# Attention units spread over more steps of token blocks 1 and 2, and the given stores moved behind the last weight load

## The chip, the core and the metric

The kernel runs on one core of a Trainium2 chip. The metric is the device time of one execution in microseconds (us), the median of three runs. The core's engines work side by side, each through its own instructions in order: TensorE (PE, matrix products), VectorE (DVE), ScalarE (ACT), GpSimd (POOL) and SyncE (SP, which here issues transfers). They wait for each other through semaphores.

## What is computed

Attention inside chunks of 64 tokens, for 8 batches, 8 heads, 576 tokens and a head width of 64, and then a gated layer over the 4608 tokens:

```python
scores = scale * np.matmul(q_c, k_c.transpose(0, 1, 2, 4, 3))    # 64 x 64 in each chunk
scores = scores - np.max(scores, axis=-1, keepdims=True)
attn = np.exp(scores)
attn = attn / (np.sum(attn, axis=-1, keepdims=True) + 1e-09)
out = np.matmul(attn, v_c)
...
x = np.ascontiguousarray(attn_out.transpose(0, 2, 1, 3)).reshape(B * S, H * D)   # 4608 x 512
gate = 1.0 / (1.0 + np.exp(-(x @ w_gate)))                       # 512 x 1536
val = x @ w_val                                                  # 512 x 1536
return (gate * val @ w_out).astype(np.float32)                   # 1536 x 512
```

## The kernel before

The 4608 tokens are nine blocks (m = 0 to 8) of 512. The attention of a block is four *units* j (4m to 4m+3), handled two at a time. The 1536 hidden columns are twelve *slices* f of 128. Each weight is held as a high and a low float part, so every product takes three matmuls per 128 rows.

**Words used below.** A *step* is `step(m, f, span)`: slice f of a block's hidden values, 12 matmuls for the gate, 12 for the value (`up`, L277), a sigmoid on ACT (L286 in block 0, L302 in blocks 1 and 2) and a product on DVE (L288 or L304). A step over all 512 tokens has 24 matmuls of 512 columns; an `a` or `b` step covers 256 tokens. *S j* is the scores' products of units j and j+1 (L172, 64 matmuls of 64 columns on PE, written `sc`); *A j* is their products with the values (L243, written `av`).

**Stages.** Block 0 runs while the weights arrive: `START` and `MIDDLE` are strings of operations run by `run(op)`. W is a weight load (L102, issued by SP), C a weight conversion (ACT L123, L124, L130; DVE L125, L126, L128, L131), H a step, D a down projection, L and V loads of q, k and v, K a store of an output weight from POOL (`keep_outer`), G two times three stores of converted up weights from SP (`keep_given`, the *given stores*). The string `MIDDLE` ends with steps of block 1 in halves: H1.0a to H1.3a, H1.0b to H1.3b. Then `singles` runs the rest of block 1 (slices 4 to 11) and all of block 2 (0 to 11), and `pair` runs the down projection of these two blocks (L660) and the later blocks in pairs.

**What sets the order.** In `MIDDLE` PE and SP keep the order of the string, while the other engines are ordered by a scheduler; in `singles` every engine keeps the written order. The attention of units 8 and up is the generator `flow()`, cut into pieces: S, two transposes (L737) that take the scores out of their banks and a maximum (L741); an exchange of halves on ACT (L720); maximum and subtraction (L745, L746) and the exponential on ACT (L748, with a table load before and one back to the sigmoid behind it); then A of the unit pair before; sums (L764), exchange, L768, reciprocal (L771), product (L772), two transposes (L776). `tick(share)` adds a credit twice in each step and runs DVE pieces as the credit pays for them; `insert(upto, 1)` runs an S, or an A of a unit below `upto`. `SHARES` holds the credit of a tick in blocks 1 and 2.

**What can wait.** The banks of `sc` and `av` are one pool of two (`psa`): A j waits until L737 has taken the scores of S j+2 out, and S waits until the results of the A before it are copied out (L263 on ACT and L264 on DVE for blocks below 3, L260 on ACT after that). The half steps of block 1 write the banks `g0` and `g1`, of which there is one each: a gate waits for the sigmoid of the step before it, a value for its L304. The full steps of blocks 1 and 2 write `acc`, of which there are four. POOL makes sums of weights (`keep_sums`: L402, L381, L384, L385 and a store) one after the other in the same stretch.

Of the kernel before, what the change touches and what calls it, by code (L numbers as in the profile page):

```python
# [16 lines left out]
D = 64  # L17
# [15 lines left out]
H0.5 D W5o L6 C5.2 L7 C6.2 H0.6 V4 W8u C7.1 D W7o C8.0 t5 C8.1 C7.2 H0.7 D K0 K6 W9u  # L33
"""
MIDDLE = """
C9.0 W8o C8.2 W9o C9.1 W10u A4 K1 K7 H0.8 W10o D C10.0 C9.2 C10.2 W11u G0 H0.9 C10.1 K2 K8 D H0.10 C11.0 G1 C11.1 D
W11o H0.11 G2 K3 K9 S7 V7 S6 D L9 E6 H1.0a C11.2 D V6 E7 H1.1a T6 T7 K4 K10 H1.2a A6 H1.3a H1.0b L8 V8 K5 K11 H1.1b V9 H1.2b H1.3b
"""

VECTOR_TRANSPOSES = 8  # L40

# [4 lines left out]

FIRST_STEP = 4

SHARES = {1: 1.7, 2: 1.8, "up": 1.0, "turned": 0.36}


@with_exitstack
def chunk_attn_moe(ctx: ExitStack, tc: tile.TileContext, q, k, v, w, out, turned_out):
# [39 lines left out]
    def load_weights(f, kind):  # L93
        if kind == "o":
            raws[f, 2] = stage("spare" if f == NF - 1 else f"o{NF - 1 if f == NF - 2 else NF - 1 - f % 2}", 1024)
        elif f == NF - 1:
            raws[f, 0], raws[f, 1] = stage(f"o{f}", 1024), stage("spare", 1024)
        else:
            raw = stage(f"u{NF - 1 if f == NF - 2 else NF - 1 - f % 2}", 2048)
            raws[f, 0], raws[f, 1] = raw[:, :1024], raw[:, 1024:]  # L100
        for part in (2,) if kind == "o" else (0, 1):
            nc.sync.dma_start(raws[f, part], w[f, :, part * 1024:(part + 1) * 1024])  # L102
# [35 lines left out]
    def load(j):  # L138
        m, h, u = units[j]
        state[j] = {}  # L140
        for name, src in (("qt", q), ("kt", k)):
            t = state[j][name] = ap2.tile([P, 2, 256], F32, name=name)
            nc.sync.dma_start(t, src[2 * m + h, u].rearrange("p (a n) -> p a n", a=2))

    def load_values(j):
        m, h, u = units[j]
        vt = ap2.tile([P, 2, 2, 2, D], F32, name="vt")
        nc.sync.dma_start(vt, v[2 * m + h, u].rearrange("p (i a t d) -> p i a t d", i=2, a=2, t=2))
        state[j]["vt"] = vt
# [29 lines left out]
    def scores(j, on_scalar=False):  # L179
        n, i = divmod(j, 2)  # L180
        if n not in pairs:
            pr = early[:, n] if n < 2 else ap2.tile([P, 2, 8, D], F32, name="pr", bufs=1)
            pairs[n] = dict(sc=products(2 * n, n == 1), pr=pr, sums={})
        s = pairs[n]
        scv, pr = s["sc"][i].rearrange("p (g k) -> p g k", k=D), s["pr"][:, i]
        mx = sm.tile([P, 8], F32, name="mx")
        nc.vector.reduce_max(out=mx, in_=scv, axis=AX.X)
        if not on_scalar:
            nc.vector.tensor_tensor(out=pr, in0=scv, in1=mx.unsqueeze(2).broadcast_to([P, 8, D]), op=ALU.subtract)
            return  # L190
        nc.vector.tensor_scalar_mul(out=mx, in0=mx, scalar1=-0.125)
        sums = s["sums"][i] = sm.tile([P, 8], F32, name="sums")
        for g in range(8):
            nc.scalar.activation(
                pr[:, g], scv[:, g], AF.Exp, scale=0.125, bias=mx[:, g:g + 1], accum_out=sums[:, g:g + 1])

    def softmax(j):
        n, i = divmod(j, 2)
        pr = pairs[n]["pr"][:, i]
        sums = pairs[n]["sums"].get(i)  # L200
        if sums is None:
            nc.scalar.activation(pr, pr, AF.Exp, scale=0.125)
            sums = sm.tile([P, 8], F32, name="sums")
            nc.vector.reduce_sum(out=sums, in_=pr, axis=AX.X)
        nc.vector.tensor_scalar_add(out=sums, in0=sums, scalar1=1e-9)
        inv = sm.tile([P, 8], F32, name="inv")
        nc.vector.reciprocal(out=inv, in_=sums)
        nc.vector.tensor_tensor(out=pr, in0=pr, in1=inv.unsqueeze(2).broadcast_to([P, 8, D]), op=ALU.mult)
# [4 lines left out]
    def transposes(j, on_scalar=False):  # L213
        n, u = divmod(j, 2)
        s = pairs[n]
        if u == 0:
            s["pt"] = turned()
        tp = bank("tp", n == 0)
        for i in range(2):
            for t in range(2):  # L220
                g = 4 * u + 2 * t
                nc.tensor.transpose(
                    tp[:, (2 * i + t) * P:(2 * i + t + 1) * P],
                    s["pr"][:, i, g:g + 2].rearrange("p c k -> p (c k)"), ident)
        pt = s["pt"][:, :, u].rearrange("p i t a q -> p i (t a q)")
        tp = tp.rearrange("p (i n) -> p i n", i=2)
        if on_scalar:
            nc.scalar.copy(pt, tp)
        else:
            nc.vector.tensor_copy(pt, tp)  # L230
# [552 lines left out]
    def advance():  # L783
        now["unit"] += 2 * (now["item"] == "A")
        now["item"] = next(ahead, None)
        now["since"] = now["ticks"]

    def tick(share):
        now["ticks"] += 1
        now["credit"] += share  # L790
        while now["item"] is not None:
            if isinstance(now["item"], float):
                if now["credit"] < now["item"] / 2:
                    return
                now["credit"] -= now["item"]
            elif not (now["item"] == "wait" and now["ticks"] > now["since"] + 1
                      or now["item"] == "next" and now["ticks"] > now["since"]
                      or now["item"][0] in ("open", "freed") and now["item"][1] <= now[now["item"][0]]):
                break
            advance()  # L800
        now["credit"] = min(now["credit"], share)

    def insert(upto=4 * NB, pieces=0):


        if now["item"] == "S" or (
                now["item"] == "A" and now["unit"] < upto and now["ticks"] >= now["since"] + pieces):
            advance()
# [9 lines left out]
    def step(m, f, span, aside=False):  # L818
        if m:
            hidden_kept(m, f, spans[span], aside)  # L820
        else:
            pending.append(hidden(m, f, spans[span]))
# [4 lines left out]
    def run(op):  # L827
        what, arg = op[0], op[1:]
        if what == "L":
            load(int(arg))  # L830
        elif what == "V":
            load_values(int(arg))
        elif what in "Ss":
            scores(int(arg), what == "s")
        elif what == "E":
            softmax(int(arg))
        elif what in "Tt":
            transposes(int(arg), what == "t")
        elif what == "A":
            values(int(arg), pairs.pop(int(arg) // 2)["pt"])  # L840
        elif what == "W":
            load_weights(int(arg[:-1]), arg[-1])
        elif what == "C":
            f, part = arg.split(".")
            convert_weights(int(f), int(part))
        elif what == "G":
            for which in range(2):
                keep_given(int(arg), which)
        elif what == "K":
            keep_outer(int(arg))  # L850
        elif what == "H":
            m, f = arg.split(".")
            step(int(m), int(f.rstrip("ab")), f.lstrip("0123456789"))
        else:
            finish()
# [12 lines left out]
    for op in START.split():  # L868
        run(op)
    def singles():  # L870
        for m in range(1, FIRST_PAIR):
            upto = 4 * (m + 2) if m == 1 else 4 * (m + 3)
            while now["unit"] < 4 * (m + 1):
                advance()
            for f in range(FIRST_STEP if m == 1 else 0, NF):
                if m == 2 and f == 7:
                    now["open"] = 0
                if m == 2 and f == NF - 1:
                    down_begin(-1)
                step(m, f, "", True)  # L880
                tick(SHARES[m])
                insert(upto, 1)
                if m == 2 and f < NF - 2:
                    down_sums(-1, f)
                tick(SHARES[m])
                insert(upto, 1)
                if givens:
                    keep_given(*givens.pop(0))
                if kept[0][2] is None:
                    keep()  # L890

    def pair(n):
# [5 lines left out]
        for i, (p, which) in enumerate(order if n >= 0 else ()):  # L898
            if i + 1 < len(order) and i > 0:
                load_group(n, *order[i + 1])  # L900
            first(n, p, which)
            tick(SHARES["up"])
            if i:
                keep(2)
                last(n, *order[i - 1])
                tick(SHARES["up"] if i < 11 else 0)
                insert(upto, 1)
                if i > 1:
                    down_sums(n, i - 2)
            middle(n, p, which)  # L910
            tick(SHARES["up"] if i < 11 else 0)
            insert(upto, 1)
# [5 lines left out]
        def between(q):  # L918
            now["freed"] = q if n < 0 else 99
            if n < LAST:  # L920
                if q in (32, 36):
                    load_group(n + 1, 0, 0, ((q - 32) // 4,))
                if n < 0 and q == 32:
                    fetch(*kept[0], nc.sync)
                tick(SHARES["turned"] if q > 3 else 0)
                insert(upto, 1)
# [46 lines left out]
```

## Time and profile before

| | |
|---|---|
| median of 3 runs | 913.88 us (912.83 to 914.04) |
| time of the profiled execution | 914.54 us |
| its span, first to last instruction | 912.8 us |
| PE busy | 876.5 us, 96% of the span |
| DVE busy | 669.3 us, 73% |
| ACT busy | 397.5 us, 44% |
| POOL busy | 243.4 us, 27% |

PE is busy nearly all of the time, so what counts is the time in which it is not, and the time in which its clock is low. Both lie in the first third of the span, and the rows further down show where. Times of rows are in us from the start of the span.

### The profile page before, as it was taken

How to read it: one execution, taken by the hardware profiler on the slowest of the kernel's cores; microseconds unless marked ns; L12 is line 12 of the kernel's file. 1: busy time of each engine (PE TensorE's matmuls, PEld its weight loads, DVE VectorE, ACT ScalarE, POOL GpSimd, SP SyncE). 2: the span in 40 equal slices, each digit the busy share in tenths (PEclk: the TensorE clock that was granted, in tenths of full speed). 3: DMA queues.
4: the chain of work that ended last, by engine and by line, in shares of the span. 5: the costliest groups of instructions: out<-in, count | busy, mean ns of one | idle time of the engine just before them, and what ended most of it. 6: DMA issues, size and time to landing. Idle time of an engine off the chain costs nothing.

```text
span 912.8 us, 15591 instructions
## 1 busy us (share of the span) xinstructions
PE 876.5 (96%) x6016; PEld 719.8 (79%) x6016; DVE 669.3 (73%) x1007; ACT 397.5 (44%) x734; POOL 243.4 (27%) x275
## 2 busy tenths in 40 slices
PE   4889999998988999999999999999999999999998
PEld 3778879887776888787887888888888888888886
DVE  6988955266777768687987896778778945565873
ACT  6989643143333645243336552432345521112640
POOL 0011226899993000898860000000000000000000
PEclk7899999999989999999999999999999999999999
DMA  8875595499774658899996677685555786565762
GB/s 310 279 267 203 169 330 195 148 337 366 273 256 136 196 178 265 302 345 355 358 309 204 210 223 273 216 265 197 200 161 176 232 282 205 169 204 160 232 207 94
DMA packets 152107, 216.53 MB, mean 237 GB/s; under 512 B 9056, under 2 KB 90464, under 8 KB 150496
## 3 DMA queue, kind: packets, MB, share of 16 engines
q1 hardware_dynamic: 143248, 178.29, 60.3%
q0 software_dynamic: 8784, 37.23, 11.0%
q8 instruction: 48, 0.79, 0.4%
q14 instruction: 27, 0.22, 0.1%
HBM read 169.87 MB, written 45.61 MB: 236 GB/s over the span
## 4 chain that ended last, share of the span: by engine, by line
PE 71%; DVE 12%; ACT 9%; DMA 6%; issue 2%; SPq 1%; ACTq 0%; DVEq 0%
PE dx L660 17%; PE cy L503 15%; PE cz L503 10%; PE cx L503 9%; PE acc L277 7%; PE dz L660 7%; DMA w_raw<-w_in 4%; PE g L277 2%; PE av L243 2%; PE sc L172 1%; ACT w_raw L123 1%; DMA wr<-sums 1%; ACT w_raw L124 1%; DVE pr L772 1%; ACT w L130 1%
## 5 line engine op out<-in xcount | busy, mean ns | idle before, releaser
L503 PE MATMUL cy<-xc,wr 128*128 128x512 f32 x648 | 159.6, 390 | 1.4 <-DMA wr<-sums 1.1
L503 PEld LDWEIGHTS cy<-xc,wr 128*128 128x128 f32 x648 | 121.4, 188 | 27.9 <-DVE mx L741 2.1
L277 PE MATMUL acc<-xt,w 128*128 128x512 f32 x480 | 116.8, 402 | 0.0
L277 PEld LDWEIGHTS acc<-xt,w 128*128 128x128 f32 x480 | 92.0, 194 | 20.1
L503 PE MATMUL cz<-xc,wr 128*128 128x512 f32 x432 | 107.2, 392 | 0.0
L503 PE MATMUL cx<-xc,wr 128*128 128x512 f32 x432 | 105.7, 391 | 0.0
L660 PE MATMUL dx<-hs,wd 128*128 128x512 f32 x432 | 101.6, 389 | 0.0
L277 PE MATMUL g<-xt,w 128*128 128x256 f32 (+1 forms) x528 | 95.5, 339 | 4.3 <-ACT hf L286 1.4
L660 PEld LDWEIGHTS dx<-hs,wd 128*128 128x128 f32 x432 | 81.1, 188 | 16.8
L503 PEld LDWEIGHTS cx<-xc,wr 128*128 128x128 f32 x432 | 80.7, 188 | 16.9
L277 PEld LDWEIGHTS g<-xt,w 128*128 128x128 f32 x528 | 81.8, 195 | 15.3 <-ACT hf L286 1.8
L503 PEld LDWEIGHTS cz<-xc,wr 128*128 128x128 f32 x432 | 80.3, 188 | 16.9
L660 PE MATMUL dx<-hx,wd 128*128 128x512 f32 x288 | 70.4, 391 | 0.4 <-DVE hx L636 0.4
L660 PEld LDWEIGHTS dx<-hx,wd 128*128 128x128 f32 x288 | 53.7, 188 | 13.2 <-DVE hx L636 1.7
L521 DVE TENSOR_TENSOR s<-cy,s 128x512 f32<-128x512 f32 x36 | 24.8, 690 | 51.0 <-PE cy L503 45.3
L635 ACT CAST hs<-hid 128x512 fp32r<-128x512 f32 x66 | 38.3, 620 | 45.8 <-PE dx L660 28.6
L519 ACT COPY s<-cx 128x512 f32<-128x512 f32 x36 | 21.2, 589 | 83.2 <-PE cx L503 83.1
L636 DVE TENSOR_TENSOR hs<-hid,hs 128x512 fp32r<-128x512 f32 x66 | 43.5, 702 | 14.9 <-ACT hs L635 14.9
L660 PE MATMUL dz<-hs,wd 128*128 128x512 f32 x216 | 51.3, 389 | 0.0
L358 POOL DMA_DIRECT2D outer<-w x24 | 18.6, 774 | 117.8 <-issue 44.2
L660 PEld LDWEIGHTS dz<-hs,wd 128*128 128x128 f32 x216 | 40.5, 188 | 8.4
L543 ACT ACTIVATE hid<-cx 128x512 f32<-128x512 f32 x18 | 10.8, 598 | 83.2 <-PE cx L503 83.1
(135 smaller groups left out, 1424.5 us busy)
## 6 DMA issues: line engine op xcount, KB each, us to landing
wr<-sums SPq DMA_DIRECT2D x72, 512.0 KB, 5.9
w_raw<-w_in SPq DMA_DIRECT2D x36, 512.0 KB, 5.3
wd<-outer SPq DMA_DIRECT2D x72, 256.0 KB, 5.4
wd<-outer_sums SPq DMA_DIRECT2D x16, 1024.0 KB, 5.6
wr<-whole SPq DMA_DIRECT2D x54, 256.0 KB, 4.6
qt<-q_in SPq DMA_DIRECT2D x36, 256.0 KB, 5.3
kt<-k_in SPq DMA_DIRECT2D x36, 256.0 KB, 5.4
vt<-v_in SPq DMA_DIRECT2D x36, 256.0 KB, 3.9
```

The costliest lines, as they stand in the source:

```text
L123: nc.scalar.mul(val.bitcast(F32), high.bitcast(F32), 2.0 ** -112)
L124: nc.scalar.mul(low, low, 2.0 ** -29)
L243: nc.tensor.matmul(av[c][a * D:(a + 1) * D, n0:n0 + D], lhsT=vt[u][rows, i, a, t, :], rhs=pt[rows, i, u, t, a, :], start=True, stop=True)
L277: nc.tensor.matmul(ps[:, tok], lhsT=wt[f, which][:, wpart, c:c + P], rhs=xt[m][:, part, 2 * u + i, tok], start=n == 0, stop=n == 11)
L358: nc.gpsimd.dma_start(outer[:, f, c], src[:, :, c])
L503: nc.tensor.matmul(bank, lhsT=lhs(wpart, c), rhs=x[:, part, c], start=start and k == 0, stop=stop and k == 5, skip_group_check=True)
L519: nc.scalar.copy(s1, x)
L521: nc.vector.tensor_tensor(out=u2, in0=y, in1=s1, op=ALU.add)
L543: nc.scalar.activation(hid[n, f][:, 0], x, AF.Sigmoid)
L635: nc.scalar.copy(hi, src)
L636: nc.vector.tensor_tensor(out=lo, in0=src, in1=hi.bitcast(F32), op=ALU.subtract)
L660: nc.tensor.matmul(bank[to][c], lhsT=down_lhs(r, f, wpart, c), rhs=down_in[q][part], start=r in (1, 6, 5) and (f, i) == (0, 0), stop=stop ...
```

## The change

The string `MIDDLE` loses its end, which becomes a string `LEAD` that `singles` runs, with a tick and an insert behind each of its steps; the two shares become smaller; the given stores G0 to G2 move behind the last weight load W11o; the loads L8, V8 and V9 and the last K stores take other places.

```diff
-C9.0 W8o C8.2 W9o C9.1 W10u A4 K1 K7 H0.8 W10o D C10.0 C9.2 C10.2 W11u G0 H0.9 C10.1 K2 K8 D H0.10 C11.0 G1 C11.1 D
-W11o H0.11 G2 K3 K9 S7 V7 S6 D L9 E6 H1.0a C11.2 D V6 E7 H1.1a T6 T7 K4 K10 H1.2a A6 H1.3a H1.0b L8 V8 K5 K11 H1.1b V9 H1.2b H1.3b
+C9.0 W8o C8.2 W9o C9.1 W10u A4 K1 K7 H0.8 W10o D C10.0 C9.2 C10.2 W11u H0.9 C10.1 K2 K8 D H0.10 C11.0 C11.1 D
+W11o H0.11 G0 K3 K9 S7 V7 S6 G1 D L9 L8 E6 H1.0a C11.2 D V6 G2 E7 H1.1a T6 T7 K4 K10 H1.2a A6 H1.3a
 """
+LEAD = "H1.0b V8 V9 K5 K11 H1.1b H1.2b H1.3b"
...
-SHARES = {1: 1.7, 2: 1.8, "up": 1.0, "turned": 0.36}
+SHARES = {1: 1.4, 2: 1.3, "up": 1.0, "turned": 0.36}
...
     def singles():
+        for op in LEAD.split():
+            run(op)
+            if op[0] == "H":
+                tick(SHARES[1])
+                insert(12, 1)
         for m in range(1, FIRST_PAIR):
```

No instruction of the computation is added or taken away; they change places. (Lines of the changed kernel are one higher than those named here, up to `singles`.) On PE, from the last half steps of block 1 on, there stood before (`g_` is a gate or value product of a half step, two in a row to a step; `acc` x24 is a full step):

```order
L277 MATMUL g_1741<-xt,w 128x256 x12
L277 MATMUL g_1755<-xt,w 128x256 x12
L277 MATMUL g_1779<-xt,w 128x256 x12
L277 MATMUL g_1793<-xt,w 128x256 x12
L277 MATMUL g_1809<-xt,w 128x256 x12
L277 MATMUL g_1823<-xt,w 128x256 x12
L277 MATMUL g_1837<-xt,w 128x256 x12
L277 MATMUL g_1851<-xt,w 128x256 x12
L277 MATMUL acc<-xt,w 128x512 x24
L172 MATMUL sc<-qt,kt 64x64 x32
L277 MATMUL acc<-xt,w 128x512 x48
L172 MATMUL sc<-qt,kt 64x64 x32
```

And now:

```order
L278 MATMUL g_1750<-xt,w 128x256 x12
L278 MATMUL g_1764<-xt,w 128x256 x12
L173 MATMUL sc<-qt,kt 64x64 x32
L278 MATMUL g_1829<-xt,w 128x256 x12
L278 MATMUL g_1843<-xt,w 128x256 x12
L278 MATMUL g_1866<-xt,w 128x256 x12
L278 MATMUL g_1880<-xt,w 128x256 x12
L278 MATMUL g_1897<-xt,w 128x256 x12
L278 MATMUL g_1911<-xt,w 128x256 x12
L278 MATMUL acc<-xt,w 128x512 x24
L173 MATMUL sc<-qt,kt 64x64 x32
L278 MATMUL acc<-xt,w 128x512 x48
```

S 8 moved up by three half steps and one full step, to behind H1.0b. From there on PE has two full steps between every S and the A behind it, and one between an A and the next S, up to A 18; before, of the six from S 10 on, three (S 12, S 16 and S 20) had one step between S and A. A 18 now stands two steps ahead of the down projection, where it stood three ahead.

On ACT, the sigmoids of the same half steps (`other` is the exchange of S 8's maxima) stood before as

```order
L302 ACTIVATE hid<-g_1779 128x256
L302 ACTIVATE hid<-g_1809 128x256
L302 ACTIVATE hid<-g_1837 128x256
L302 ACTIVATE hid<-acc 128x512
L720 COPY other<-mx_1944 32x32 x4
```

and stand now as

```order
L303 ACTIVATE hid<-g_1829 128x256
L721 COPY other<-mx_1859 32x32 x4
L303 ACTIVATE hid<-g_1866 128x256
L749 ACT_TABLE_LOAD
L749 ACTIVATE pr<-pr 128x1024
L303 ACT_TABLE_LOAD
L303 ACTIVATE hid<-g_1897 128x256
```

The exchange of S 8 stands between the sigmoids of H1.1b and H1.2b, and the exponential between those of H1.2b and H1.3b.

On SP, around the last weight load (the lone or last `w_raw`, W11o), there stood before

```order
L102 DMA w_raw<-w_in 128x1024 x14
L347 DMA given_1283<-w 128x2x256 x3
L347 DMA given_1287<-w 128x2x256 x3
L347 DMA given_1388<-w 128x2x256 x3
L347 DMA given_1392<-w 128x2x256 x3
L102 DMA w_raw<-w_in 128x1024
L347 DMA given_1450<-w 128x2x256 x3
```

and now

```order
L103 DMA w_raw<-w_in 128x1024 x15
L348 DMA given_1434<-w 128x2x256 x3
L348 DMA given_1438<-w 128x2x256 x3
L149 DMA vt<-v_in 128x512
L348 DMA given_1489<-w 128x2x256 x3
L348 DMA given_1493<-w 128x2x256 x3
```

Twelve given stores no longer stand ahead of W11o. With this the scheduler gave ACT another order at the conversion C11.2 that waits for W11o; before, the sigmoid of H0.10 (`g_1347`) stood ahead of it:

```order
L286 ACTIVATE hf<-g_1347 128x512
L123 ACTIVATE w_val<-w_raw 128x512
L124 ACTIVATE w_raw<-w_raw 128x512
L291 CAST hx<-hf 128x512
L130 CAST w<-w_val 128x512
L286 ACTIVATE hf<-g_1418 128x512
```

and now the sigmoid of H0.10 (`g_1339`) stands behind the whole of it:

```order
L124 ACTIVATE w_raw<-w_raw 128x512
L131 CAST w<-w_val 128x512
L287 ACTIVATE hf<-g_1339 128x512
L292 CAST hx<-hf 128x512
L287 ACTIVATE hf<-g_1402 128x512
```

## Rows read from the trace of the kernel before

**Rows 1.** Windows: per stretch, busy per engine, granted PE clock, DMA share, GB/s

```profile
250.00:260.00 10.00, 6.12 (x73) 5.04 (x74) 8.26 (x11) 3.38 (x7) 9.18 (x9) 0.67 0.71 247
```

**Rows 2.** Waits of PE, 60 to 320 us: total, times, longest

```profile
PE av L243 <- DVE pr L737: 7.9, 5, 3.8
PE sc L172 <- DVE xt L264: 1.8, 2, 1.5
...
PE g L277 <- DVE hf L288: 1.4, 1, 1.4
PE sc L172 <- ACT raw L260: 0.5, 2, 0.3
```

**Rows 3.** Timeline of PE: start, duration, what, [idle before and its releaser]

```profile
128.93 2.88 PE L277 MATMUL g<-xt,w 128*128 128x512 f32 x12
...
154.15 14.65 PE L277 MATMUL g<-xt,w 128*128 128x256 f32 x120
...
174.20 1.16 PE L172 MATMUL sc<-qt,kt 64*64 64x64 f32 x64
175.29 11.18 PE L277 MATMUL acc<-xt,w 128*128 128x512 f32 x48
...
222.64 1.91 PE L172 MATMUL sc<-qt,kt 64*64 64x64 f32 x62 [0.27 <-DVE xt L264]
224.48 11.95 PE L277 MATMUL acc<-xt,w 128*128 128x512 f32 x48
...
253.76 2.58 PE L243 MATMUL av<-pt,vt 64*64 64x64 f32 x64 [3.81 <-DVE pr L737]
256.26 7.61 PE L277 MATMUL acc<-xt,w 128*128 128x512 f32 x24
...
295.02 17.94 PE L277 MATMUL acc<-xt,w 128*128 128x512 f32 x72
```

**Rows 4.** Chain that ended last, by time, around the last weight loads

```profile
112.36 3.80 DMA w_raw<-w_in
...
120.65 0.61 DVE w_val L128
...
124.43 6.27 DMA w_raw<-w_in
```

**Rows 5.** Timeline of SP's queue, the given stores ahead of W11o

```profile
113.22 11.10 SPq L347 DMA_DIRECT2D given<-w  x12
```

**Rows 6.** Timeline of ACT

```profile
118.17 0.68 ACT L123 ACTIVATE w_val<-w_raw 128x512 f32<-128x512 f32 x1 [0.69 <-DVE w_val L126]
...
121.29 0.62 ACT L130 CAST w<-w_val 128x512 fp32r<-128x512 f32 x1 [0.86 <-DVE w_val L128]
...
196.58 0.90 ACT L720 COPY other<-mx 32x32 f32<-32x32 f32 x4 [5.43 <-DVE mx L741]
...
198.99 1.06 ACT L748 ACTIVATE pr<-pr 128x1024 f32<-128x1024 f32 x1 [0.22 <-DVE pr L746]
...
201.86 1.07 ACT L263 CAST xt<-av 128x512 fp32r<-128x512 f32 x2
```

**Rows 7.** Timeline of DVE

```profile
160.27 0.42 DVE L304 TENSOR_TENSOR hid<-g,hid 128x256 f32<-128x256 f32 x1 [2.47 <-PE g L277]
...
193.93 1.30 DVE L737 STREAM_TRANSPOSE pr<-sc 128x512 f32<-128x512 f32 x2
195.27 1.22 DVE L741 TENSOR_REDUCE mx<-pr 128x32 f32<-128x1024 f32 x1
...
197.73 1.23 DVE L746 TENSOR_TENSOR pr<-pr,mx 128x1024 f32<-128x1024 f32 x1
...
235.28 2.41 DVE L745 TENSOR_TENSOR mx<-mx,other 128x32 f32<-128x32 f32 x1 [0.42 <-ACT other L720]
...
297.14 0.18 DVE L745 TENSOR_TENSOR mx<-mx,other 128x32 f32<-128x32 f32 x1
```

**Rows 8.** Timeline of POOL, at the long L745 of rows 7

```profile
235.11 2.52 POOL L402 TENSOR_TENSOR a_val<-again 128x512 f32<-128x512 f32 x2
```

## Prediction

> **What bounds the kernel now.** I read the windows first, then the waits of PE in the stretch that the change touches, then PE's timeline there, and last the order of the changed kernel. PE is the bound, but not everywhere: in the worst ten microseconds of blocks 1 and 2 it is busy for 6.12 of 10 us, at a granted clock of 0.67 [rows 1]. The waits name the cause: A waits for L737, the DVE transposes that empty the score banks (7.9 us in all, up to 3.8), S waits for the copies that empty the value banks (1.8 and 0.5), and one step of block 0 waits 1.4 us for L288 [rows 2]. Together 11.6 us.
>
> Behind three of these waits the clock falls to its lower level, and PE's timeline shows the price [rows 3]. An S takes 1.16 us and two steps 11.18 (5.59 each) at full clock. After the wait at 222 the S took 1.91 and the two steps 11.95: 0.75 + 0.77 lost. After the wait of 3.81 us the A took 2.58 (it has as many matmuls as an S) and the step 7.61: 1.42 + 2.02. At 295.02 three steps took 17.94 against 16.77: 1.17. That is 6.1 us. So 11.6 + 6.1 = 17.7 us can be won between 129 and 313 us. The later blocks follow the same order as before, and I let the gain pass through to the end unchanged.
>
> **The regular cycle (gain).** In the changed order every cycle is S, two steps, A, one step. Set S at 0: the steps end at 6.7 and 12.3, A at 13.4, the next S is due at 19.0. A needs the L737 of the new scores. DVE runs them behind L304 of the first step (an estimate of 0.7 us, from 0.42 for half the width [rows 7]), so they are done at 6.7 + 0.7 + 1.30 = 8.7, some 3.6 us before A asks. Before, three of the A had only one step there, and the transposes then ended after PE was through. So I take the 7.9 us of A's waits as gone, with the clock falls behind them.
>
> The next S is nearer. From 12.3 on: L304 0.7, L745 0.18, L746 1.23 [rows 7], the exponential 1.06, the copies out of the value banks 1.07 [rows 6], and 0.7 for the last L264 on DVE: 17.3 with the small gaps, against 19.0. That leaves 1.7 us for A 8 and A 10; later A's have ACT copies alone, 2.4 us, of which a late L304 can take some. What eats it is DVE's contact with POOL: L745 is 0.18 us on a quiet chip and took 2.41 where it began beside POOL's L402, until that had ended [rows 7, 8]. Over the five cycles A 8 to A 16 I leave 0.8 us of waits (0 to 5: none, or 1 us in every cycle).
>
> The Trainium skill, "GPSIMD Engine Reference", § Key points, says that GpSimd shares its SBUF interfaces with VectorE and contends with DVE instructions that read two SBUF inputs; L745, L746 and L772 are such. The trace agrees (2.41 against 0.18 us). The rule speaks against the change, which brings more of these instructions per microsecond next to POOL's sums; what it would make of the time is a rival below.
>
> **S 8 among the half steps (loss).** This is a wait that the trace before doesn't have. The half steps own one gate bank, so the gate of H1.3b waits for the sigmoid of H1.2b, and that now stands behind the exchange of S 8's maxima on ACT. In the times of the trace: five half steps take 14.65 us [rows 3], 2.9 each. From 154.15: H1.3a and H1.0b end at 159.95, S 8 lets H1.1b start at 161.05 (starts follow at 1.1), which ends at 163.95. L304 starts 0.3 later, as at 160.27, and its successor 0.35 after that [rows 7]: L737 164.6 to 165.9, L741 (1.22) to 167.15, the exchange (0.90 [rows 6]) from 167.25 to 168.15, the sigmoid of a half step (taken at L304's 0.42) to 168.55. PE had H1.2b done at 163.95 + 2.9 = 166.85. The wait is **1.7 us** (1.5 to 2.0: nothing on DVE or ACT there is optional). The full steps behind it write other banks, so the long exponential costs nothing.
>
> **The given stores (gain, mostly).** SP issued twelve of them for 11.10 us from 113.22 on [rows 5], and W11o only then, at 124.43, landing 6.27 us later [rows 4]. Its staging buffer was free at 121.26, when L128 ended [rows 4]. Now SP issues at 121.3. The landing I bound by 3.80 (112.36, ahead of the stores [rows 4]) and 6.27; I take 4.3, near the low end, because the queue ahead is empty as it was for that load: landed at 125.6. But the sigmoid of H0.10 now stands behind C11.2 on ACT. From the first L123 to the end of L130 took 3.74 us a conversion earlier (118.17 to 121.91 [rows 6]), 0.6 of it a foreign L131; with the sigmoid (0.6) that is some 3.75 again. So the gate bank is free at 129.35, and PE asks at 128.93 [rows 3]: **0.4 us** (0 to 2.4) in place of the 1.4. The twelve stores then stand ahead of loads that are due tens of microseconds later, so I cost them at nothing; the cover is gone if a load of v stands behind them, and the one for A 6 keeps its place behind the output stores.
>
> "DMA: Bandwidth & Descriptors", § Issuing engines are not separate DMA queues, in the Trainium skill says that transfers of SP and POOL interleave on the same 16 engines. By that, POOL's K stores still slow W11o; a landing of 6.27 would be the fourth rival's time.
>
> **The start of the down projection (loss).** A 18 now has two steps behind it, not three, and DVE and ACT must do the same work in 11.2 us: after the last step's L304 come two operations on 1024 columns (L480, L493; estimated at L741's 1.22) and then the split of the fourth operand (0.7). With A 18 ending at 13.4 in the cycle's frame, the down projection starts at 24.6 and wants the fourth operand's low part at 28.9. The ACT row of three conversions (1.06 each, estimated by the exponential on as many columns) and three half as long delays the last sigmoid to 25.4; L304 ends at 26.2, L480 and L493 at 28.65, the cast behind the fourth conversion comes at 29.1 and the low part at 29.75. Wait **0.8 us** (0 to 1.5).
>
> **Clock.** The new 1.7 us wait is as long as the wait before the S at 222 (1.5 + 0.27 us [rows 2, 3]), after which the clock fell. I take one fall among all the new waits, at the 1.5 us that the S at 222 paid (0 to 3.0).
>
> **Sum.** New: 0.8 + 1.7 + 0.4 + 0.8 + 1.5 = 5.2 us. Gain 17.7 − 5.2 = 12.5 us. The profiled execution took 914.54 us, its span 912.8; less 12.5 it is 902.0. The median of the runs is 0.66 lower (913.88), so I predict 913.88 − 12.5 = **901.4 us**.
>
> **Rivals.** (1) *The new waits find cover:* all but the 1.7 us go, and no clock falls. 17.7 − 1.7 = 16.0 won, 897.9 us. For it: slack of 1.7 to 3.6 us in the cycle. Against: the down projection's margin is negative on paper. (2) *POOL holds DVE in two cycles:* two long hits of 2.2 us in one cycle leave the next S some 2 us late, and the clock falls (1.5): 3.5 a cycle. Two cycles cost 7.0 in place of the 0.8, so 11.4 new, 6.3 won, 907.6 us. Three cycles give 911.1. (3) *The same in all five cycles, slower than before:* 17.5 + 4.4 = 21.9 new against 17.7, 918.1 us. It turns at 17.7 − 4.4 = 13.3 us, four cycles (14.0, 914.6, no change) being just past it. Against it: with a less regular order, PE's waits for the value banks came to only 2.3 us in the trace [rows 2]. (4) *The earlier issue brings nothing:* W11o lands 6.27 us after issue, PE waits 2.4 instead of 0.4: 903.4 us.
>
> **How the numbers follow.** Forecast 0.53; rival 1: 0.20; rival 2 with two or three cycles 0.15; rival 4: 0.07; four cycles 0.02; five 0.03. The range 897.5 to 907.5 holds the forecast, rivals 1 and 4 and the lower edge of rival 2, and the unknown terms' ends unless several fall together. A measurement of this kernel tells about 0.2% (1.8 us) from no change: faster than that 0.95, within it 0.02, slower 0.03.
>
> **What would show it.** In the new trace A's wait for L737 should be under 1 us in total; a wait of PE for the sigmoid L303, 1.5 to 2 us, should stand at H1.3b, close to 167 us; the wait for the value banks should be under 2 us; the down projection should start near 300 us, not 313; from there on the time to the end should be the same. I am wrong if DVE rows near POOL's grow past 2 us in most cycles, if the clock falls three times again, or if the later blocks give the time back.

## The result, and the profile after

The changed kernel took 905.18 us (median of 4 runs, 904.30 to 906.32) against 913.96 us of the kernel before in the same comparison: a ratio of 0.9898, 95% interval 0.9869 to 0.9928. The forecast of 901.4 us (897.5 to 907.5) had the sign and held the time in its range; the gain is 8.8 us where 12.5 were forecast. The profiled execution took 904.59 us, its span 902.8.

Lines of the changed kernel stand one higher than in the rows of before (the sigmoid L302 is now L303, L737 is L738, L304 L305, L243 L244, L660 L661). First, from the pages of the two kernels, the granted clock in 40 slices, before:

```profile
PEclk7899999999989999999999999999999999999999
```

and after:

```profile
PEclk7999999999999999999999999999999999999999
```

Behind the start there is no slice below 9, and in stretches of 5 us the granted clock is 1.00 from 60 us to 900 us: the clock falls of [rows 3] are all gone. The window that was worst before [rows 1], same columns:

```profile
250.00:260.00 10.00, 8.74 (x97) 6.97 (x96) 6.93 (x7) 5.24 (x10) 9.27 (x10) 1.00 0.79 284
```

PE is busy for 8.74 us in place of 6.12, at full clock in place of 0.67. The waits of PE from 60 to 320 us (total, times, longest), which answer to [rows 2]:

```profile
PE dx L661 <- ACT hs L636: 2.7, 1, 2.7
PE g L278 <- ACT hid L303: 1.5, 1, 1.5
PE sc L173 <- ACT raw L261: 1.4, 3, 1.1
PE av L244 <- PE acc L278: 0.6, 1, 0.6
PE g L278 <- ACT hf L287: 0.4, 1, 0.4
PE dx L661 <- ACT hx L636: 0.4, 1, 0.4
PE av L244 <- DVE pr L738: 0.3, 1, 0.3
...
```

A's wait for the transposes fell from 7.9 us to 0.3 (1.0 with the piece of 0.63 put down to the accumulation L278 just ahead of it). A new group stands at the top that the kernel before has not in this stretch: `dx`, the first product of the down projection, waits for the split of its operands (L636 on ACT, and L637 on DVE with 0.2 us each). PE's timeline (start, duration, what, [idle before and its releaser]) shows the places, as [rows 3] did:

```profile
127.92 5.73 PE L278 MATMUL g<-xt,w 128*128 128x512 f32 x24 [0.44 <-ACT hf L287]
...
165.92 3.14 PE L278 MATMUL g<-xt,w 128*128 128x256 f32 x24 [1.52 <-ACT hid L303]
...
285.38 1.16 PE L244 MATMUL av<-pt,vt 64*64 64x64 f32 x62 [0.35 <-DVE pr L738]
286.47 11.17 PE L278 MATMUL acc<-xt,w 128*128 128x512 f32 x48
300.35 0.49 PE L661 MATMUL dx<-hs,wd 128*128 128x512 f32 x1 [2.71 <-ACT hs L636]
301.07 2.79 PE L661 MATMUL dx<-hs,wd 128*128 128x512 f32 x11 [0.23 <-DVE hs L637]
...
305.62 0.50 PE L661 MATMUL dx<-hx,wd 128*128 128x512 f32 x1 [0.39 <-ACT hx L636]
306.34 1.45 PE L661 MATMUL dx<-hx,wd 128*128 128x512 f32 x5 [0.22 <-DVE hx L637]
307.63 2.90 PE L661 MATMUL dx<-hs,wd 128*128 128x512 f32 x12
...
313.09 2.88 PE L661 MATMUL dx<-hs,wd 128*128 128x512 f32 x12
```

The first two rows are the terms for the given stores (forecast 0.4 us) and for S 8 among the half steps (forecast 1.7), close to the forecast in this execution. The start of the down projection is not: 2.71 + 0.23 + 0.39 + 0.22 = 3.55 us of waits where 0.8 was forecast.

**Where the 8.8 us went.** Set matmul against matmul in the two profiled executions, the changed kernel is already 1.6 us ahead at 49.8 us, where the two orders are still the same; that belongs to these two executions. At the first `dx` it is 12.45 us ahead (300.35 against 312.80), 10.8 without the 1.6. The waits for the split operands behind the first one cost 1.8 us of it, read from start to start (7.28 us for the first 24 `dx`, 5.44 before), and near 413 us PE waits 1.80 us for the sums that it reads back where it waited 1.12 at that matmul before:

```profile
412.82 3.00 PE L504 MATMUL cy<-xc,wr 128*128 128x512 f32 x12 [1.80 <-DMA wr<-sums]
```

At the end 8.4 us of lead are left without the 1.6, close to the medians' 8.8; differences of some tenths elsewhere go both ways.

### The profile page after: what moved, and what is told of

It is laid out like the page before. It is cut to its first block, busy times and chain, and to the rows that moved or that the text cites. A ratio compares the mean times of both kernels' runs of the same rounds, so it can differ in the third digit from the quotient of the medians.

```text
span 902.8 us, 15594 instructions
## 1 busy us (share of the span) xinstructions
PE 869.1 (96%) x6016; PEld 711.7 (79%) x6016; DVE 674.6 (75%) x1007; ACT 397.4 (44%) x734; POOL 244.4 (27%) x275
## 4 chain that ended last, share of the span: by engine, by line
PE 63%; DMA 1%; DVE 1%; ACT 1%; issue 1%; SPq 0%; ACTq 0%; DVEq 0%
PE dx L661 17%; PE cy L504 16%; PE cz L504 11%; PE cx L504 10%; PE dz L661 7%; DMA wr<-sums 1%; PE av L244 1%; PE sc L173 1%; DVE hx L637 0%; ACT hx L636 0%; SPq L144 0%; DVE raw L481 0%; ACT xc L485 0%; DVE hid L685 0%; ACT hs L636 0%
## 5 line engine op out<-in xcount | busy, mean ns | idle before, releaser
L278 PE MATMUL acc<-xt,w 128*128 128x512 f32 x480 | 112.6, 392 | 0.0
L661 PE MATMUL dx<-hs,wd 128*128 128x512 f32 x432 | 102.1, 390 | 2.9 <-ACT hs L636 2.7
L278 PEld LDWEIGHTS acc<-xt,w 128*128 128x128 f32 x480 | 89.1, 188 | 18.9
L278 PE MATMUL g<-xt,w 128*128 128x256 f32 (+1 forms) x528 | 94.7, 335 | 7.0 <-ACT hf L287 2.6
L661 PEld LDWEIGHTS dx<-hs,wd 128*128 128x128 f32 x432 | 81.0, 188 | 20.5 <-ACT hs L636 3.1
L278 PEld LDWEIGHTS g<-xt,w 128*128 128x128 f32 x528 | 80.0, 190 | 18.9 <-ACT hf L287 3.7
L661 PE MATMUL dx<-hx,wd 128*128 128x512 f32 x288 | 71.1, 393 | 1.1 <-DVE hx L637 0.7
L661 PEld LDWEIGHTS dx<-hx,wd 128*128 128x128 f32 x288 | 53.7, 188 | 14.6 <-DVE hx L637 2.2
L636 ACT CAST hs<-hid 128x512 fp32r<-128x512 f32 x66 | 38.3, 620 | 43.7 <-PE dx L661 26.5
L637 DVE TENSOR_TENSOR hs<-hid,hs 128x512 fp32r<-128x512 f32 x66 | 43.6, 703 | 13.8 <-ACT hs L636 13.8
L661 PE MATMUL dz<-hs,wd 128*128 128x512 f32 x216 | 51.2, 389 | 0.0
L544 ACT ACTIVATE hid<-cx 128x512 f32<-128x512 f32 x18 | 10.8, 598 | 83.3 <-PE cx L504 83.3
L661 PEld LDWEIGHTS dz<-hs,wd 128*128 128x128 f32 x216 | 40.5, 188 | 8.4
```

The costliest lines, as they stand in the source:

```text
L278: nc.tensor.matmul(ps[:, tok], lhsT=wt[f, which][:, wpart, c:c + P], rhs=xt[m][:, part, 2 * u + i, tok], start=n == 0, stop=n == 11)
L544: nc.scalar.activation(hid[n, f][:, 0], x, AF.Sigmoid)
L636: nc.scalar.copy(hi, src)
L637: nc.vector.tensor_tensor(out=lo, in0=src, in1=hi.bitcast(F32), op=ALU.subtract)
L661: nc.tensor.matmul(bank[to][c], lhsT=down_lhs(r, f, wpart, c), rhs=down_in[q][part], start=r in (1, 6, 5) and (f, i) == (0, 0), stop=stop ...
```

## Theories and experiments

**Theory A** (POOL): DVE operations that read two SBUF inputs wait for POOL's sums, so DVE and ACT come late to the end of the last cycle, and the down projection pays. **Theory B** (order): the operands of the next group (`xc`: L481, L485, L494), which `now["open"] = 0` lets in behind A 18, two steps ahead of the down projection, stand ahead of the split on ACT and DVE, and that alone makes the wait. **Theory C** (spacing): A 18 has two steps behind it and not three; a step more would remove the wait. The other kernels take the parts of the change apart. Times are medians; these runs were on three chips, and the kernel before took 917.54 us beside e1 to e4, 912.89 beside a0, e9, e6 and e7, and 916.01 beside e8 and e10. So between these three sets only the ratios compare.

### e1: the attention alone, given stores back at their places

```
-... W11u H0.9 C10.1 K2 K8 D H0.10 C11.0 C11.1 D
-W11o H0.11 G0 K3 K9 S7 V7 S6 G1 D L9 L8 E6 H1.0a C11.2 D V6 G2 E7 ...
+... W11u G0 H0.9 C10.1 K2 K8 D H0.10 C11.0 G1 C11.1 D
+W11o H0.11 G2 K3 K9 S7 V7 S6 D L9 L8 E6 H1.0a C11.2 D V6 E7 ...
```

> The changed kernel with the given stores G0 to G2 put back where they stood. Theory: the move is worth what PE's timeline shows near 130 us, a wait of 1.4 us for L288 before and 0.44 us for the sigmoid after, so this one is about 1 us slower than the changed kernel (some 906 us), with the 1.4 us wait back and everything from the lead steps on as in the changed kernel. Rival: the stores also hold the lead and the later loads; then the waits at H1.3b or at the value loads move too, by over 0.5 us, and the loss is 2 us or more.

906.84 us, ratio 0.9897 (0.9862 to 0.9931), not to be told from the changed kernel's 0.9898. Its waits in the attention cycles are close to those of the changed kernel (1.52 us for the sigmoid, S 0.7, 2.70 at the down projection). Behind the last of these the clock fell, as it did not in the changed kernel:

```profile
302.66 4.65 PE L661 MATMUL dx<-hs,wd 128*128 128x512 f32 x12 [2.70 <-ACT hs L636]
```

From the first product behind A 4 to the first behind A 6 it took 50.4 us against 48.7 for the changed kernel. Nearly all of that is a wait of 1.83 us for A 6's values (0.26 in the changed kernel), which also turned up in kernels that have the stores moved (e4 1.87, e9 1.76, e7 1.71), so it is not the stores' doing. The 1.4 us wait that was expected back at H0.10 came to 0.54 us. The attention's spread carries most of the gain; with the spread in place, what the stores add is not shown by the times.

### e2: the given stores alone

```
-... W11u G0 H0.9 C10.1 K2 K8 D H0.10 C11.0 G1 C11.1 D
-W11o H0.11 G2 K3 K9 S7 V7 S6 D L9 E6 H1.0a C11.2 D V6 E7 ...
+... W11u H0.9 C10.1 K2 K8 D H0.10 C11.0 C11.1 D
+W11o H0.11 G0 K3 K9 S7 V7 S6 G1 D L9 E6 H1.0a C11.2 D V6 G2 E7 ...
```

> The kernel before with the given stores moved behind W11o and nothing else. Theory: about 1 us faster than the kernel before (0.9990 of its time), with A's waits for L738 or L737 of some 8 us and the three clock falls still there. Rival: the wait moves to the value load of A 6 and nothing is gained.

913.61 us, ratio 0.9952 (0.9928 to 0.9976). The same stretch took 48.1 us against 49.9 before: 1.8 won there, since the waits of 1.41 us at H0.10 and of 0.49 for A 6's values are gone. For the whole kernel the interval means 2.2 to 6.6 us, more than the 1 us that was expected and more than this stretch shows; where the rest came from is open. A's waits for L737 are all back (8.8 us, five times, up to 4.0) and the clock falls behind them, as at the longest:

```profile
252.39 2.58 PE L243 MATMUL av<-pt,vt 64*64 64x64 f32 x64 [4.05 <-DVE pr L737]
```

So this wait is the old cycle's, as [rows 3] have it, and the stores have no part in it.

### e3: POOL's sums left out

```
-            val = wp.tile([P, 4, 2, P], F32, tag="spare", name="a_val")
...
-                nc.gpsimd.tensor_tensor(out=dst, in0=x[:, 0], in1=x[:, 1], op=ALU.add)
+            both = sb.tile([P, 4, 2, 2, P], F32R, tag="a_both", name="a_both")
+            nc.gpsimd.memset(both.bitcast(F32), 0.0)
...
-            winograd(val)
-            parts([both[:, :, :, a] for a in range(2)], val)
```

> The changed kernel without the sums that POOL makes in blocks 1 and 2: each is replaced by one memset and the same store, so part of the computation is left out, while DVE, ACT, PE and SP run the same instructions. Theory A (DVE waits beside POOL, the chain of maximum, exponential and copies gets late, and the down projection finds it late): the waits of S and of A 18 go to zero, the wait at the start of the down projection falls from 3.5 us to about the 0.8 us of the forecast, and the time to 900 to 901 us. Theory B (the order alone: three conversions stand ahead of the first split on ACT, whatever POOL does): the start of the down projection still waits 2.5 us or more, and the time stays at 903 us or above.

899.77 us, ratio 0.9809 (0.9777 to 0.9841), below that of the changed kernel with no overlap. Waits of PE, 60 to 330 us (later lines stand 10 lower here, so L651 is the changed kernel's L661):

```profile
PE g L278 <- ACT hid L303: 1.5, 1, 1.5
PE g L278 <- ACT hf L287: 1.4, 1, 1.4
PE sc L173 <- DMA kt<-k_in: 1.4, 2, 0.8
PE dx L651 <- ACT hx L626: 0.3, 1, 0.3
PE dx L651 <- DVE hx L627: 0.2, 1, 0.2
```

The sums are missing from this kernel's result; what counts here is only its time. No A waits, no S waits for the value banks (it waits for loads of k instead), and the down projection starts with no wait and pays 0.35 + 0.22 = 0.57 us at its fourth operand: the place and about the size (0.8) that the prediction had worked out. The 1.5 us at S 8's exchange stays, since POOL is not in that chain. The groups of DVE between 165 and 285 us (line, tile, shape, count, busy, mean ns) show what POOL does. L765, L769 and L773 are L764, L768 and L772 of before; L613, L616 and L617 are differences of hidden values that the down projection needs (`down_sums`). The changed kernel:

```profile
L769 DVE SCALAR_TENSOR_TENSOR sums<-sums,other 128x32 f32<-128x32 f32 x6 | 10.2, 1696 | 3.6 <-ACT other L721 3.6
L773 DVE TENSOR_TENSOR pr<-pr,sums 128x1024 f32<-128x1024 f32 x6 | 9.8, 1633 | 0.2
...
L613 DVE TENSOR_TENSOR t<-hid 128x512 f32<-128x512 f32 x6 | 8.9, 1480 | 0.0
L738 DVE STREAM_TRANSPOSE pr<-sc 128x512 f32<-128x512 f32 x12 | 7.8, 685 | 0.0
L765 DVE TENSOR_REDUCE sums<-pr 128x32 f32<-128x1024 f32 x6 | 7.2, 1208 | 0.0
```

and e3 (L759 is L769, L763 is L773, L603 is L613, L728 is L738, L755 is L765):

```profile
L759 DVE SCALAR_TENSOR_TENSOR sums<-sums,other 128x32 f32<-128x32 f32 x6 | 1.1, 191 | 3.9 <-ACT other L711 3.9
L763 DVE TENSOR_TENSOR pr<-pr,sums 128x1024 f32<-128x1024 f32 x6 | 7.4, 1225 | 0.2
L603 DVE TENSOR_TENSOR t<-hid 128x512 f32<-128x512 f32 x6 | 4.0, 672 | 0.0
L728 DVE STREAM_TRANSPOSE pr<-sc 128x512 f32<-128x512 f32 x12 | 7.8, 690 | 0.0
L755 DVE TENSOR_REDUCE sums<-pr 128x32 f32<-128x1024 f32 x6 | 7.3, 1209 | 0.0
```

The 32-column update of the sums takes 1.70 us on average beside POOL and 0.19 without it; the two-input operations on 512 and 1024 columns grow by 0.4 to 0.8 us; transposes and reductions, with one input, do not grow at all. The long instruction ends when POOL's does, as in [rows 7] and [rows 8]. In the changed kernel's last cycle DVE has

```profile
273.74 0.69 DVE L305 TENSOR_TENSOR hid<-acc,hid 128x512 f32<-128x512 f32 x1 [0.61 <-ACT hid L303]
...
275.47 1.24 DVE L616 TENSOR_TENSOR t<-hid,t 128x512 f32<-128x512 f32 x1
276.64 1.52 DVE L617 TENSOR_TENSOR hid<-hid 128x512 f32<-128x512 f32 x1
278.08 2.38 DVE L769 SCALAR_TENSOR_TENSOR sums<-sums,other 128x32 f32<-128x32 f32 x1
...
286.33 1.21 DVE L742 TENSOR_REDUCE mx<-pr 128x32 f32<-128x1024 f32 x1
```

and POOL

```profile
277.70 2.71 POOL L386 TENSOR_TENSOR a_both<-a_val,a_both 128x1024 fp32r<-128x1024 f32 x1
```

L769 starts at 278.08 and ends at 280.46, with POOL's L386 (280.41). It and the two rows ahead of it take 5.14 us; on e3's prices (0.67, 0.68 and 0.19) they would take 1.5, so 3.6 us are lost there. The product L305 ahead of them was late already: it starts 2.4 us behind the end of its step on PE (271.3), where e3 has 0.1, because the cycle before had made ACT's sigmoid late. Together, less an idle 0.7 us that e3 has there, the transposes L738 come some 5 us later behind that step than in e3. The maxima L742 then start 1.0 us behind A 18 (at 285.38), where e3 starts them 2.3 us ahead of its A 18, and ACT's row passes this on (ACT's timeline of the changed kernel):

```profile
291.27 1.06 ACT L749 ACTIVATE pr<-pr 128x1024 f32<-128x1024 f32 x1 [0.81 <-DVE pr L747]
...
293.30 1.28 ACT L303 ACT_TABLE_LOAD   x1
294.60 0.60 ACT L303 ACTIVATE hid<-acc 128x512 f32<-128x512 f32 x1
295.09 1.99 ACT L485 CAST xc<-raw 128x1024 fp32r<-128x1024 f32 x2
298.73 1.04 ACT L485 CAST xc<-raw 128x1024 fp32r<-128x1024 f32 x1 [1.64 <-issue]
299.68 1.13 ACT L636 CAST hs<-hid 128x512 fp32r<-128x512 f32 x2
```

POOL has no row behind 281.4 here. What it held up earlier arrives at PE 20 us later, at 300.35. Theory A stands: the exponential, the sigmoid L303 behind its table load, the conversions and the split L636 follow each other on ACT, each as late as the maxima made the first. From the exponential to the split this chain takes 8.4 us here (291.27 to 299.68) and in e3 (286.42 to 294.80): it starts late, it is not slower. The 1.64 us ahead of the third conversion are part of it both times (1.60 in e3): ACT waits for DVE's L481, which ends at 298.65.

The Trainium skill, "GPSIMD Engine Reference", § Key points, states this contention of GpSimd with VectorE instructions that have two SBUF inputs; the trace agrees (1.70 us against 0.19).

### e4: the operands opened behind the first splits of the down projection

```
-                if m == 2 and f == 7:
-                    now["open"] = 0
                 if m == 2 and f == NF - 1:
                     down_begin(-1)
+                    now["open"] = 0
```

> The changed kernel with the conversions of the next pair (operands) opened only behind the splits of the down projection, so that ACT's first splits no longer stand behind three conversions. Theory A: the splits are made as soon as slice 10's products allow it, the first product of the down projection waits for nothing, some 0 to 1 us is left at the fourth operand behind the conversions, and the time falls by 2.5 to 3.5 us to about 902 us; A 18's wait of 1 us stays. Theory B expects the same there. Rival: the conversions are then late for the fourth operand or for the next pair, which waits as long as the first product did, and the time stays at 905 us.

906.92 us, ratio 0.9870 (0.9829 to 0.9912), not to be told from the changed kernel's. The wait at the first `dx` is gone; PE's waits at the start of the down projection are now

```profile
PE dx L661 <- ACT hx L636: 0.8, 1, 0.8
PE dx L661 <- ACT hs L636: 0.7, 1, 0.7
```

with 0.2 for each of the two L637: 1.9 us in place of 3.55. So the order does decide what waits: of the lateness that POOL causes, 1.7 us can be hidden behind products whose operands are there. Theory B holds as far as that, and falls as the whole cause, because e3 keeps the early opening and waits 0.57. The 3.55 us need both, POOL's hold and the conversions ahead of the split.

### a0: the changed kernel again, beside e9, e6 and e7

> The changed kernel once more, unchanged, on the chip of the next three. Both theories: the ratio 0.990 to the kernel before; at H1.3b a wait of 1.5 us for the sigmoid; at the start of the down projection 3 to 4 us in all; A 18 about 1 us; no fall of the clock between 60 and 900 us, or one at the start of the down projection. What differs from run to run should be the landings of transfers (the wait for k near 45 us, the value load of A 6).

905.45 us, ratio 0.9917 (0.9894 to 0.9941). The main waits repeat: 1.52 us for the sigmoid, 2.71 + 0.23 + 0.38 + 0.23 at the down projection, S 0.8, A 1.2, and no fall of the clock. The small ones do not: H0.10 waits for nothing (0.44 in the first profile), and near 413 us PE waits 0.87 us for a given weight and 0.33 for the sums.

### e9: S 8 half a step earlier, the exchange of its maxima a step later on ACT

```
-... K4 K10 H1.2a A6 H1.3a
+... K4 K10 H1.2a A6
-LEAD = "H1.0b V8 V9 K5 K11 H1.1b H1.2b H1.3b"
+LEAD = "H1.3a H1.0b V8 V9 K5 K11 H1.1b H1.2b H1.3b"
...
+                if j == 8:
+                    yield "next"
                 other = exchange(mx)
```

> The changed kernel with S 8 half a step earlier (behind H1.3a) and the exchange of its maxima one step later on ACT, behind the sigmoid of H1.1b, which by then has nothing to wait for; everything from the first full step on stands as in the changed kernel. Theory of the forecast (the gate of H1.3b waits because the sigmoid of H1.2b stands behind the exchange): the wait of 1.5 us is gone and nothing takes its place, 1.5 us less than the changed kernel on the same chip. Rival (the single gate bank is the limit wherever the exchange stands): a wait of 1 us or more is found at another half step, and the time is that of the changed kernel.

904.25 us, ratio 0.9908 (0.9886 to 0.9930). The 1.52 us at the sigmoid are gone, which fits the forecast's cause, the exchange ahead of the sigmoid on ACT; S 8's own place moved with it, and the two were not tried apart. By the medians 1.2 us came back (905.45 to 904.25; the intervals overlap). The down projection waits 2.68 us, and there the clock fell:

```profile
302.25 5.79 PE L661 MATMUL dx<-hs,wd 128*128 128x512 f32 x12 [2.68 <-ACT hs L636]
```

### e6: e9, and everything from S 10 on a step earlier

```
+        for _ in range(2):
+            tick(SHARES[1])
+            insert(12, 1)
...
-                insert(upto, 1)
+                insert(16 if m == 1 and f == NF - 1 else upto, 1)
```

> As the last one, with two more ticks at the end of the lead and A 12 allowed behind the last step of block 1: from S 10 on, every S and A stands one full step earlier, so that A 18 has three steps behind it before the down projection, and there are still two steps between S and A. Theory A (the chain that POOL makes late is 4 to 5 us late at A 18, and a third step of 5.6 us covers it): the wait at the start of the down projection falls to under 1 us, the waits of S and A stay at 1 to 2.5 us, and the time is 4 to 5 us under the changed kernel's on the same chip, about 0.985 of the kernel before. Rival: the lateness is not of a fixed size but grows with each cycle; then S 20 or A 18 waits longer and the gain is under 2 us.

904.48 us, ratio 0.9913 (0.9892 to 0.9935): no gain on e9. With three steps behind A 18 the first wait at the down projection halves, S 20 pays instead, and the clock falls behind the shorter wait too:

```profile
269.94 0.33 PE L173 MATMUL sc<-qt,kt 64*64 64x64 f32 x2 [2.31 <-ACT raw L261]
...
301.69 0.50 PE L661 MATMUL dx<-hs,wd 128*128 128x512 f32 x1 [1.35 <-ACT hs L636]
302.42 4.16 PE L661 MATMUL dx<-hs,wd 128*128 128x512 f32 x11 [0.23 <-DVE hs L637]
```

The S waits sum to 3.7 us against 1.7 in e9. Theory C falls: the lateness is work that DVE and ACT don't get done beside POOL, and a step more of distance moves it to the next place that asks.

### e7: the changed kernel with the old shares

```
-SHARES = {1: 1.4, 2: 1.3, "up": 1.0, "turned": 0.36}
+SHARES = {1: 1.7, 2: 1.8, "up": 1.0, "turned": 0.36}
```

> The changed kernel with the old credits per tick (1.7 and 1.8): S 8 is still among the half steps, but in three of six pairs there is again only one step between S and A. Theory (the number of steps between S and A decides A's wait): the three A with one step wait for L738 as in the kernel before, 7 to 9 us in all, with the clock falling behind at least one, and the down projection, which now has four steps behind the last A, waits for nothing; about 908 to 911 us. Rival (starting the units earlier is what helps, whatever the spacing): A's waits stay under 2 us and the time under 903 us.

911.14 us (one run, 912.89 before). The lead is kept, but the work runs ahead in larger portions, and the waits at the regular places are back while the down projection has none:

```profile
PE av L244 <- DVE pr L738: 4.3, 5, 2.0
PE sc L173 <- ACT raw L261: 3.4, 4, 2.0
```

Behind the S of 274 us and the A of 285 us, which each waited 2.0 us, the granted clock is 0.66 over 5 us. So the spacing is what the shares buy, S and A at even distances; the lead alone would not have done it. This rests on one run, and on the waits of its trace.

### e8: e9 with e4's late opening

> The late exchange of S 8 and the late opening of the conversions together. Theory: the two savings lie at different places of PE's path (1.5 us at H1.3b, 1.7 us at the start of the down projection) and add: 2.5 to 3.5 us under the changed kernel, 0.988 to 0.989 of the kernel before on this chip, some 902 us where the changed kernel takes 905. Rival (DVE, held by POOL, bounds the stretch of blocks 1 and 2, and PE waits for it in one place or the other): what is saved at H1.3b comes back at S 16, S 20 or the down projection, and the time is within 1 us of the late exchange alone.

902.80 us (6 runs, 901.91 to 904.06), ratio 0.9850 (0.9822 to 0.9878): the lowest beside e3. The changed kernel had 0.9898 and 0.9917; the interval overlaps that of the first (from 0.9869) by little and that of a0 (from 0.9894) not at all. So the two moves together very likely bring time, by the ratios 4 to 6 us. No A waits for the transposes, and the 1.52 us for the sigmoid are gone; S waits 2.4 us, the down projection 0.76 + 0.22 + 0.64 + 0.23 = 1.85:

```profile
302.92 0.50 PE L661 MATMUL dx<-hx,wd 128*128 128x512 f32 x1 [0.76 <-ACT hx L636]
```

### e10: e8 with A 6's value load issued earlier

```
-W11o H0.11 G0 K3 K9 S7 V7 S6 G1 D L9 L8 E6 H1.0a C11.2 D V6 G2 E7 ...
+W11o H0.11 G0 K3 K9 S7 V7 V6 S6 G1 D L9 L8 E6 H1.0a C11.2 D G2 E7 ...
```

> As the last one, with the value load of unit 6 moved from behind the output stores to right behind that of unit 7. Theory: A 6's wait for it (0.3 us in the profile of the changed kernel, 1.7 to 1.9 in four of the others) is gone in every run; 0.3 to 1.5 us less than the last one. Rival: the sums of POOL and all later loads start with PE, so the chain that DVE makes late is as late as before and takes the gain back at the down projection.

903.89 us, ratio 0.9865 (0.9834 to 0.9896). A 6 no longer waits for its values, but in e8's trace that wait was only 0.35 us, so there was little to win. S (1.9) and A (1.0) wait at later places, and the time is not below e8's. Whether a longer wait saved at A 6 would come back later is not shown.

## Why the prediction was right, and where it was off

**The cause and its cure: right.** With two steps between S and A the transposes L738 are done when A asks: 7.9 us became 1.0 at most in the first trace and 1.2 in a0. e1, e2 and e7 show that lead and spacing did it, not the stores.

**S 8 among the half steps: right, 1.52 us for 1.7**, again 1.52 in a0, and gone in e9. PE resumed at 165.92, where "close to 167 us" was said.

**The given stores: the landing right, the price partly luck.** W11o was issued at 119.7 us, and its first conversion started at 124.0: 4.3 us, the value taken (4.0 in a0, 4.2 in e2). Rival 4, a landing as long as before, is out. The wait at H0.10, 0.44 us for 0.4, fits so well by chance: the same kernel had none there in a0, and with the stores back it was 0.54 in e1 and not 1.4. Alone the move gains (e2); beside the spread its gain is not told from nothing (e1).

**The S waits: 0.8 forecast, 1.42 measured** (0.8 in a0), within the bounds given. One sign of being wrong came true all the same: between 165 and 312 us the changed kernel has seven DVE rows of more than 2 us, in most cycles. The kernel before has six and e3 none, so they are POOL's, but they were there already: as a sign they could not tell the two apart. In the cycles they cost PE little; their price came behind the last one.

**Clock: 1.5 us forecast, none lost.** The reason given was the likeness of the 1.52 us wait to the one at the S of 222 us; no fall followed it, nor the 2.71 us wait. In both traces of the changed kernel the term was too dear. But in e1 and e9, behind 2.70 and 2.68 us at the same `dx`, and in e6 behind 1.35, the clock did fall: from 300 to 310 us the granted clock was 0.83, 0.66 and 0.83, against 1.00 in the changed kernel. So one fall among the new waits was a fair guess, but the 1.52 us wait that it was reasoned from had none in any trace.

**The start of the down projection: the step that failed.** The term was mis-sized, 0.8 us against 3.55 of waits (the clock term's error of 1.5 us the other way hides half of that in the sum). Its working took A 18 and the exponential ahead of it as on time, and its one place for POOL's hold on DVE was the S of the regular cycles. Behind S 20 no S follows: the lateness of that last cycle has nowhere to show but at the first `dx`. e3 comes close to the forecast's own number (0.57 against 0.8) when POOL is taken out; e6 shows that distance only moves the place. POOL's hold should have been charged to each thing that DVE delivers to, the last one included. Rival 2 had POOL as its mechanism and expected it as S waits in two cycles with clock falls; the mechanism was at work, its place and price were not those.

**The rest of the time: nearly.** "Let the gain pass through" gave back 0.7 us at the sums read back near 413 us. It is the landing of a transfer that differs, and it differs from trace to trace: 1.12 us before, 1.80 in the changed kernel, 0.33 in a0, 0.49 in e2, none in e1. What sets it was not tried.

**The sum.** With what was measured in place of the terms: waits of 1.4 (S), 1.0 (A), 1.5 (S 8), 0.4 (H0.10) and 3.6 (down projection) are 7.9 us, so 17.7 − 7.9 = 9.8; less 0.7 given back, and less about 1 us that the split starts of `dx` cost beyond their waits, 8.1, against 8.8 by the medians and 8.4 in the trace. What stays open is under 1 us, less than the 1.6 us by which the two executions differ before the change begins.

## What to carry to other kernels

When work of a helper engine is spread out to cover waits in a regular cycle, follow the last cycle to the consumer behind it: lateness that each cycle passes on shows where the pattern ends, and there it has its price. Charge one engine's hold on another to everything the held engine delivers, not to the one wait where it was seen. And once the helper engines are short of time, moving their tasks earlier (e6) changes which wait shows; moving a task that nobody waits for yet behind one that PE waits for (e4 and e9) takes that wait away, and the two together (e8) bring time, where neither alone is told from the changed kernel.

## What was unexpected of the hardware

- One of the smallest DVE operations lost the most beside POOL: the 128x32 update L769 took 1.70 us on average, up to 2.89 (1.12 on average in a0), against 0.19 without POOL's sums, while one-input operations of 1024 columns kept their 1.21 us. Size does not decide it: L746, as small, stayed at 0.18 in five of its seven rows of the first trace and took 2.46 once in a0.
- A stop costs PE more than the idle time that a row shows. From start to start the first 24 `dx` took 307.63 − 300.35 = 7.28 us, the next 24 took 313.09 − 307.63 = 5.46; the waits in between are only 0.84 of the 1.8 us lost.
- Nearly equal waits at the same matmul had different outcomes for the clock: after 2.71 us the changed kernel ran on at full clock (11 `dx` in 2.79 us), after 2.68 us e9 did not (12 in 5.79), nor after 2.70 us e1 (12 in 4.65). These runs don't say what decided.
